# A delta-rule attention handed out in smaller pieces between the matmuls of a dense layer

## The chip, the cores and the metric

The kernel runs on one core of one Trainium2 chip. The metric is the device time of one execution in microseconds. Engines are named as in the profile: PE (TensorE matmuls), PEld (its weight loads), DVE (VectorE), ACT (ScalarE), POOL (GpSimd), SP (SyncE, which issues the DMAs).

## The reference

Three parts run one after the other on 4 x 768 tokens.

```
k_n = k / (norm(k) + 1e-6)                       # attention: B=4, H=8, S=768, D=48
for t in range(S):
    y[t] = q[t] @ state                          # per batch and head, state is D x D
    state += beta[t] * outer(k_n[t], v[t] - k_n[t] @ state)
x = y as (3072, 384)
x2 = leaky(x @ w_in, 0.01) @ w_out               # first dense layer, 384 -> 2048 -> 384
P = exp(x2 @ w_gate - max), 8 rounds of row and column normalising
out = sum_e P[:, e] * (relu(x2 @ w1[e]) @ w2[e]) # 8 experts, 384 -> 1024 -> 384
```

The arithmetic is that of 32-bit floats. Dense products are made of three products of a high and a low part each.

## The kernel before, in words

Time is cut into NT = 6 chunks of C = 128 tokens. For each chunk the recurrence becomes a triangular system per batch and head. `part1(t)` normalises k, makes its transpose (`kt_ps`), the products of k with itself (`g_ps`, two banks a batch) and their fp16 parts (`nh`, `nl`). `solve(t)` inverts the 32 x 32 (in chunks 0 and 1 the 16 x 16) diagonal blocks on DVE. `part2(t, b)` does one batch of one chunk: the masked products of k and q (`m_ps`, two halves), then the blocks `x` of the inverse, then levels that double the inverted blocks (s = 32 and 64; in chunks 0 and 1 also 16). A level is a first product (L284), ACT copies of it (L287), and the second products (L290, L294) with their copies. After the levels come a correction (`p_ps`, two pieces), `u_ps` (two pieces), the subtraction of the state's part from v (`ks_ps`), then w = u v (`w_ps`, 8 heads, L337), y (`y_ps`: the state's part L343 and the chunk's own part L346) and the state's update (`s_ps`, L354, with two DVE adds).

All three are Python generators. A `yield` marks the end of a piece, and a piece is what is handed out at once. `main_a(t)` runs the first dense layer on chunk t: 16 steps of 128 hidden columns over 512 tokens, each step three slots of three matmuls of `ph` (L503) and three slots of three matmuls of `po` (L555, for the step before). Chunk 0 has 20 steps, since its first LEAD = 4 hidden blocks go over two batches at a time. After each slot the loop gives credit: `ru` pieces from the queue of `part2` of chunk t + 1 (`bgq`, up to three generators in turn), `rs` from the queue of `part1(t + 2)` and `solve` (`bgs`), and in chunk 0 `rc` conversions. Shares are given by quarters (chunk 0: by sixths) of the step in `RATES` and `RATES0`. Before the next chunk's first step, `need_x1` hands out whatever is left of its `part2`, without slots between, and `make_x1` transposes y (L481). A batch b waits for batch b - 2, so two batches are open together, and both wait for `solve` of their chunk. `solve(t + 2)` waits for `part2` of chunk t + 1.

The weights of the first layer arrive as 64-bit floats. `convert()` turns 48 pieces of them into high and low parts on ACT, DVE and POOL (L431 to L460) and writes them to scratch in DRAM, from where `stage_a` reads them; where a step's weights are not converted yet, `stage_a` hands out the missing conversions itself. Both DMAs are issued by SP.

Ahead of the first step stands a start: `part1(0)`, `solve(0)`, and then a loop of 14 rounds (L619) that hands out one piece each of `part2(0, 0)`, `part2(0, 1)`, `part1(1)` and one conversion.

PSUM: `bank()` gives banks to the attention. In the start there are six, afterwards three (`bg`); two belong to `ph`, three to `po`. A bank comes free when its last reader is done.

The order in which a piece is handed out is a priority. A planner with its own costs puts the instructions of each engine into their order when the program is built; what it holds for not yet ready, it lets later ready work overtake. The experts run in an order that is written out by hand.

Of the kernel before, what the change touches and what calls it, by code (L numbers as in the profile page):

```python
# [8 lines left out]
F32 = mybir.dt.float32  # L9
# [4 lines left out]
ACTF = mybir.ActivationFunctionType  # L14
ALU = mybir.AluOpType
# [3 lines left out]
B, H, S, D = 4, 8, 768, 48  # L19
# [3 lines left out]
DM = H * D  # L23
# [18 lines left out]

STIR = (145, 20)

RATES0 = ((0.65, 0.3, 0.1), (0.7, 0.5, 0), (0.7, 0.45, 0), (1.05, 0.8, 0.4), (0.7, 0.35, 0), (1.05, 0, 0))
RATES = ((0.7, 0.5, 0), (0.7, 0.5, 0), (0.7, 0.5, 0), (0.7, 0.7, 0))


@with_exitstack
def delta_moe_kernel(ctx: ExitStack, tc: tile.TileContext, k_l, v_l, q_l, beta_l, wa_in, wg, wc, out):  # L50
# [3 lines left out]
    pe, act, dve, pool, sp = nc.tensor, nc.scalar, nc.vector, nc.gpsimd, nc.sync  # L54
# [21 lines left out]
    a1_p = attn_stack.enter_context(tc.tile_pool(name="a1", bufs=1, side="right"))  # L76
# [41 lines left out]
    def bank(name):  # L118
        if early is not None and early:
            early[0] += 1  # L120
            i = early[0] % 6
            if i >= 3:
                return po_p.tile([128, 512], F32, tag=f"po{i - 3}", name=name)
        return bg_p.tile([128, 512], F32, tag="bg", name=name)
# [3 lines left out]
    ybuf = {}  # L128
# [119 lines left out]
    def part2(t, b):  # L248
# [3 lines left out]
        mt = at_p.tile([128, H, C], F32, tag="mt", name="mt")  # L252
# [22 lines left out]
        for s in (16, 32, 64) if t in SMALL else (32, 64):  # L275
            pt = p1[b % 2]
            nb = C // (2 * s)

            def half(ap, odd):
                return ap.rearrange("p h (n two s) -> p h n two s", two=2, s=s)[:, :, :, odd, :]  # L280

            ps = bank("l_ps").rearrange("p (h n s) -> p h n s", h=H, n=nb)
            for h in range(H):
                marks.append(pe.matmul(out=ps[:, h], lhsT=nh[:, h, :], rhs=half(u, 1)[:, h], start=True, stop=True))  # L284
            for i in range(nb):
                o = 2 * s * i
                act.activation(out=pt[o:o + s, :, o + s:o + 2 * s], in_=ps[o:o + s, :, i, :], func=ACTF.Copy)  # L287
            ps = bank("l_ps").rearrange("p (h n s) -> p h n s", h=H, n=nb)
            for h in range(H):
                pe.matmul(out=ps[:, h], lhsT=x[:, h, :], rhs=half(pt, 1)[:, h], start=True, stop=True)  # L290
            if s > 16:
                ps2 = bank("l_ps").rearrange("p (h n s) -> p h n s", h=H, n=nb)
                for h in range(H):
                    pe.matmul(out=ps2[:, h], lhsT=pt[:, h, :], rhs=half(x, 0)[:, h], start=True, stop=True)  # L294
            for i in range(nb):
                o = 2 * s * i
                act.activation(out=u[o:o + s, :, o + s:o + 2 * s], in_=ps[o:o + s, :, i, :],  # L297
                               func=ACTF.Copy, scale=-1.0)
                if s > 16:
                    act.activation(out=x[o + s:o + 2 * s, :, o:o + s], in_=ps2[o + s:o + 2 * s, :, i, :],  # L300
                                   func=ACTF.Copy, scale=-1.0)
            if s == 16:
                dve.transpose(out=x.rearrange("p a b -> p (a b)"), in_=u.rearrange("p a b -> p (a b)"))
            yield
# [30 lines left out]
        ps = bank("w_ps")  # L335
        for h in range(H):
            pe.matmul(out=ps[:, h * D:(h + 1) * D], lhsT=uc[:, h, :], rhs=v[:, h, :], start=True, stop=True)  # L337
        act.activation(out=w, in_=ps[:, 0:DM].rearrange("p (h d) -> p h d", h=H), func=ACTF.Copy)
        yield
        ps = bank("y_ps")  # L340
        if t > 0:
            for p in range(NP):
                pe.matmul(out=ps[:, p * 2 * D:(p + 1) * 2 * D], lhsT=q[0:112, p, :],  # L343
                          rhs=st[0:112, b * NP + p, :], start=(p == 0), stop=False, skip_group_check=True)
        for h in range(H):
            pe.matmul(out=ps[:, h * D:(h + 1) * D], lhsT=mt[:, h, :], rhs=w[:, h, :],  # L346
                      start=(t == 0 and h == 0), stop=(h == H - 1), skip_group_check=True)
        y = a1_p.tile([128, DM], F32, tag=f"y{b}", name="y")
        act.activation(out=y, in_=ps[:, 0:DM], func=ACTF.Copy)
        ybuf[t, b] = y  # L350
        if t < NT - 1:
            ps = bank("s_ps").rearrange("p (n m) -> p n m", m=128)
            for p in range(NP):
                pe.matmul(out=ps[0:112, p, 0:2 * D],  # L354
                          lhsT=kn[:, 2 * p:2 * p + 2].rearrange("p a d -> p (a d)")[:, 0:112],
                          rhs=w[:, 2 * p:2 * p + 2].rearrange("p a d -> p (a d)"), start=True, stop=True)
            for o, c in ((0, 0), (64, D)):
                sv = st[o:o + D, b * NP:(b + 1) * NP, c:c + D]
                dve.tensor_tensor(out=sv, in0=sv, in1=ps[o:o + D, :, c:c + D], op=ALU.add)
        yield  # L360


# [213 lines left out]
    if True:  # L576
# [39 lines left out]
        run(s0)  # L616
        done.add(("s", 0))
        run(p1_1, 6)
        for _ in range(14):  # L619
            run(a0, 1)  # L620
            run(a1, 1)
            with tc.issue_after(solved[0].ins):
                run(p1_1, 1)
            run(cv_gen, 1)
# [459 lines left out]
```

## Time and profile before

| | us |
|---|---|
| median of three runs | 2488.13 |
| the runs | 2497.22, 2481.90, 2488.13 |
| profiled execution | 2491.82 |
| its span | 2489.8 |
| PE busy in the span | 2374.4 (95%) |
| DVE, ACT, POOL busy | 1263.4, 1162.8, 937.5 |

The stages, by the copies of the first layer's result (L560), are: the start to about 106 us, chunk 0 of the first layer to 320, chunks 1 to 4 to 847, chunk 5 with the first tiles of the experts to 940, and the experts to the end. In a row of the waits the left name is the instruction that waited and the right one what released it. Where these two share no operand, the wait is for a buffer. In a row of windows the clock is the share of TensorE's full clock that was granted; 0.50 is the lower of its two levels.

### The profile page before, as it was taken

The numbers are of one execution on the slowest core, as the hardware profiler recorded it, in microseconds if no ns is written. First come the engines' busy times: TensorE is split into PE (matmuls) and PEld (weight loads), VectorE is DVE, ScalarE is ACT, GpSimd is POOL, SyncE is SP. The second block draws the span as 40 slices with busy tenths as digits, with TensorE's granted clock in tenths as the row PEclk, the third lists the DMA queues.
The fourth block names the chain that finished last, engine by engine and source line by source line (L and its number), as shares of the span: only waits on it lengthen the run. The fifth ranks groups of instructions, "written<-read, shape, count | busy, mean of one in ns | idle before, by whom it ended". The sixth has DMA issues, their size and how long they took to land.

```text
span 2489.8 us, 35427 instructions
## 1 busy us (share of the span) xinstructions
PE 2374.4 (95%) x13836; PEld 2087.3 (84%) x13836; DVE 1263.4 (51%) x2320; ACT 1162.8 (47%) x2121; POOL 937.5 (38%) x966
## 2 busy tenths in 40 slices
PE   6788899999999999999999999999999999999999
PEld 5776677877877777899999999999999999999998
DVE  8567846446362357644444454444444544444444
ACT  6887666564654544433333344333333443333332
POOL 6435312132322213444434444444444443444441
PEclk7689999989899999999999999999999999999999
DMA  3355552424233552111111131111111311111111
GB/s 117 122 172 181 185 174 94 142 92 142 82 126 129 165 174 76 51 51 46 49 46 51 52 102 51 46 51 51 49 48 51 96 45 51 51 51 46 50 51 38
DMA packets 108695, 214.83 MB, mean 86 GB/s; under 512 B 11504, under 2 KB 79728, under 8 KB 108528
## 3 DMA queue, kind: packets, MB, share of 16 engines
q1 hardware_dynamic: 108528, 212.58, 27.5%
q8 instruction: 108, 1.77, 0.3%
q14 instruction: 59, 0.48, 0.1%
HBM read 190.43 MB, written 22.02 MB: 85 GB/s over the span
## 4 chain that ended last, share of the span: by engine, by line
PE 77%; ACT 10%; DVE 7%; issue 3%; DMA 2%; POOL 2%; SPq 0%; ACTq 0%; POOLq 0%; DVEq 0%
PE ye L964 32%; PE ph L880 13%; PE w L880 5%; PE y L880 5%; PE z L880 5%; PE ph L503 4%; PE po L555 4%; PE y_ps L346 2%; ACT x L271 2%; PE w_ps L337 2%; ACT a_d L205 1%; ACT p L287 1%; PE g_ps L189 1%; ACT u L297 1%; DVE tm L237 1%
## 5 line engine op out<-in xcount | busy, mean ns | idle before, releaser
L745 POOL TENSOR_TENSOR w2l<-stg,w2h 128x768 fp32r<-128x768 f32 x96 | 182.2, 1898 | 454.2 <-ACT w2h L744 454.2
L734 POOL TENSOR_TENSOR w1l<-stg,w1h 128x384 fp32r<-128x384 f32 x192 | 271.4, 1436 | 184.7 <-ACT w1h L733 167.2
L977 DVE SCALAR_TENSOR_TENSOR acc<-ye,pm,acc 128x384 f32<-128x384 f32 x168 | 103.5, 616 | 435.4 <-PE ye L964 435.4
L731 POOL TENSOR_TENSOR stg<-stg 128x128 f32<-128x128 f32 x384 | 209.0, 565 | 305.5 <-DMA stg<-wc 284.5
L890 ACT ACTIVATE xc<-ph 128x512 f32<-128x512 f32 x96 | 57.5, 599 | 448.5 <-PE ph L880 345.3
L555 PE MATMUL po<-gh,w 128*128 128x512 f32 (+1 forms) x600 | 217.3, 406 | 2.9 <-ACT gh L543 2.8
L880 PE MATMUL ph<-xoh,w1h 128*128 128x512 f32 x480 | 193.1, 402 | 4.7 <-DVE q L895 3.1
L503 PE MATMUL ph<-x1h,w 128*128 128x512 f32 (+1 forms) x600 | 186.7, 418 | 8.9 <-DVE leak L541 4.4
L895 DVE TENSOR_TENSOR q<-q,ph 128x512 f32<-128x512 f32 x192 | 132.2, 688 | 121.8 <-PE ph L880 121.8
L880 PE MATMUL ph<-xoh,w1l 128*128 128x512 f32 x480 | 188.1, 392 | 0.0
L880 PE MATMUL ph<-xol,w1h 128*128 128x512 f32 x480 | 187.7, 391 | 0.0
L733 ACT ACTIVATE w1h<-stg 128x384 fp32r<-128x384 f32 x192 | 121.1, 680 | 116.8 <-DMA stg<-wc 82.7
L541 DVE TENSOR_TENSOR leak<-leak,ph 128x512 f32<-128x512 f32 (+1 forms) x100 | 66.3, 663 | 165.7 <-ACT leak L540 165.5
L503 PEld LDWEIGHTS ph<-x1h,w 128*128 128x128 f32 x600 | 113.2, 202 | 32.5 <-DMA w<-wa_scratch 5.9
L555 PEld LDWEIGHTS po<-gh,w 128*128 128x128 f32 x600 | 115.4, 196 | 25.6 <-ACT gh L543 5.5
L545 POOL TENSOR_TENSOR gl<-leak,gh 128x512 fp32r<-128x512 f32 x48 | 62.1, 1294 | 192.4 <-ACT gh L543 174.7
L555 PE MATMUL po<-gl,w 128*128 128x512 f32 (+1 forms) x300 | 120.2, 401 | 3.8 <-POOL gl L545 2.3
L895 DVE TENSOR_TENSOR c<-xc,y 128x512 f32<-128x512 f32 x96 | 66.0, 688 | 106.2 <-PE y L880 83.1
L880 PEld LDWEIGHTS ph<-xoh,w1h 128*128 128x128 f32 x480 | 90.2, 188 | 34.4 <-DVE h31l L909 6.8
L880 PEld LDWEIGHTS ph<-xoh,w1l 128*128 128x128 f32 x480 | 90.2, 188 | 19.5
L540 ACT ACTIVATE leak<-ph 128x512 f32<-128x512 f32 (+1 forms) x100 | 57.8, 578 | 96.5 <-PE ph L503 93.8
L880 PEld LDWEIGHTS ph<-xol,w1h 128*128 128x128 f32 x480 | 90.3, 188 | 14.2
(316 smaller groups left out, 6683.7 us busy)
## 6 DMA issues: line engine op xcount, KB each, us to landing
w<-wa_scratch SPq DMA_DIRECT2D x100, 768.0 KB, 4.3
stg<-wc SPq DMA_DIRECT2D x192, 384.0 KB, 3.3
raw<-wa SPq DMA_DIRECT2D x48, 256.0 KB, 3.0
wa_scratch<-cvp SPq DMA_DIRECT2D x48, 256.0 KB, 2.5
stg<-x_scratch SPq DMA_DIRECT2D x10, 768.0 KB, 4.7
q<-q_l SPq DMA_DIRECT2D x24, 256.0 KB, 2.7
v<-v_l SPq DMA_DIRECT2D x24, 192.0 KB, 2.4
x_scratch<-x2o SPq DMA_DIRECT2D x18, 256.0 KB, 3.8
```

The source lines that it names most:

```text
L503: pe.matmul(out=ps, lhsT=wt[:, c * 128:(c + 1) * 128], rhs=xx[:, c], start=(n == 0), stop=(n == 3 * KD - 1))
L541: dve.tensor_tensor(out=g, in0=g, in1=ps, op=ALU.max)
L545: (dve if t in (0, 1, NT - 1) else pool).tensor_tensor(out=gl, in0=g, in1=fr(gh), op=ALU.subtract)
L555: pe.matmul(out=po[c][:, cols], lhsT=wt[:, DM + c * 128:DM + (c + 1) * 128], rhs=xx, start=(i == 1 and m == 0), stop=(i == n and m == 2), ...
L731: pool.tensor_tensor(out=s[:, o], in0=s[:, x], in1=s[:, y], op=op)
L733: ordered(act.activation(out=hi[:, j], in_=s[:, i], func=ACTF.Copy))
L734: pool.tensor_tensor(out=lo[:, j], in0=s[:, i], in1=fr(hi[:, j]), op=ALU.subtract)
L745: pool.tensor_tensor(out=lo, in0=s, in1=fr(hi), op=ALU.subtract)
L880: ordered(pe.matmul(out=ps, lhsT=w[:, a], rhs=x[:, b].rearrange("p s k -> p (s k)"), start=first, stop=i == 2 and (a, b) == terms[-1], ski ...
L895: ordered(dve.tensor_tensor(out=c, in0=x, in1=y, op=op))
L964: ordered(pe.matmul(out=ps[:, 0:DM], lhsT=xx[:, o:o + 128], rhs=wt, start=(f == 0 and i == 0), stop=(f == NF2 - 1 and i == 2), skip_group_ ...
L977: dve.scalar_tensor_tensor(out=a, in0=y, scalar=pm[:, t * B + b, e:e + 1], in1=a, op0=ALU.mult, op1=ALU.add)
```

## The change

A level's second products become a piece of their own. w is handed out as heads 0 to 2, 3 to 5, and 6 and 7 with the copy and the state's part of y; y's own part as heads 0 to 2, 3 to 5, and 6 and 7 with the copy. The state's update comes between the two parts of y, as its own piece, instead of behind y. With that `part2` has 19 pieces in chunks 2 to 4 instead of 12, 21 instead of 13 in chunks 0 and 1, and 18 instead of 12 in chunk 5. The first entries of the shares rise from 0.65, 0.7 and 1.05 to 0.95, 1.0 and 1.5. The start's loop has 22 rounds instead of 14, which also hand out 22 conversions instead of 14. No instruction is added or taken away.

```
--- before.py
+++ after.py
@@ -42,8 +42,8 @@
 
 STIR = (145, 20)
 
-RATES0 = ((0.65, 0.3, 0.1), (0.7, 0.5, 0), (0.7, 0.45, 0), (1.05, 0.8, 0.4), (0.7, 0.35, 0), (1.05, 0, 0))
-RATES = ((0.7, 0.5, 0), (0.7, 0.5, 0), (0.7, 0.5, 0), (0.7, 0.7, 0))
+RATES0 = ((0.95, 0.3, 0.1), (1.0, 0.5, 0), (1.0, 0.45, 0), (1.5, 0.8, 0.4), (1.0, 0.35, 0), (1.5, 0, 0))
+RATES = ((1.0, 0.5, 0), (1.0, 0.5, 0), (1.0, 0.5, 0), (1.0, 0.7, 0))
 
 
 @with_exitstack
@@ -285,6 +285,7 @@
             for i in range(nb):
                 o = 2 * s * i
                 act.activation(out=pt[o:o + s, :, o + s:o + 2 * s], in_=ps[o:o + s, :, i, :], func=ACTF.Copy)
+            yield
             ps = bank("l_ps").rearrange("p (h n s) -> p h n s", h=H, n=nb)
             for h in range(H):
                 pe.matmul(out=ps[:, h], lhsT=x[:, h, :], rhs=half(pt, 1)[:, h], start=True, stop=True)
@@ -335,28 +336,33 @@
         ps = bank("w_ps")
         for h in range(H):
             pe.matmul(out=ps[:, h * D:(h + 1) * D], lhsT=uc[:, h, :], rhs=v[:, h, :], start=True, stop=True)
+            if h % 3 == 2:
+                yield
         act.activation(out=w, in_=ps[:, 0:DM].rearrange("p (h d) -> p h d", h=H), func=ACTF.Copy)
-        yield
         ps = bank("y_ps")
         if t > 0:
             for p in range(NP):
                 pe.matmul(out=ps[:, p * 2 * D:(p + 1) * 2 * D], lhsT=q[0:112, p, :],
                           rhs=st[0:112, b * NP + p, :], start=(p == 0), stop=False, skip_group_check=True)
-        for h in range(H):
-            pe.matmul(out=ps[:, h * D:(h + 1) * D], lhsT=mt[:, h, :], rhs=w[:, h, :],
-                      start=(t == 0 and h == 0), stop=(h == H - 1), skip_group_check=True)
-        y = a1_p.tile([128, DM], F32, tag=f"y{b}", name="y")
-        act.activation(out=y, in_=ps[:, 0:DM], func=ACTF.Copy)
-        ybuf[t, b] = y
+        yield
         if t < NT - 1:
-            ps = bank("s_ps").rearrange("p (n m) -> p n m", m=128)
+            ss = bank("s_ps").rearrange("p (n m) -> p n m", m=128)
             for p in range(NP):
-                pe.matmul(out=ps[0:112, p, 0:2 * D],
+                pe.matmul(out=ss[0:112, p, 0:2 * D],
                           lhsT=kn[:, 2 * p:2 * p + 2].rearrange("p a d -> p (a d)")[:, 0:112],
                           rhs=w[:, 2 * p:2 * p + 2].rearrange("p a d -> p (a d)"), start=True, stop=True)
             for o, c in ((0, 0), (64, D)):
                 sv = st[o:o + D, b * NP:(b + 1) * NP, c:c + D]
-                dve.tensor_tensor(out=sv, in0=sv, in1=ps[o:o + D, :, c:c + D], op=ALU.add)
+                dve.tensor_tensor(out=sv, in0=sv, in1=ss[o:o + D, :, c:c + D], op=ALU.add)
+            yield
+        for h in range(H):
+            pe.matmul(out=ps[:, h * D:(h + 1) * D], lhsT=mt[:, h, :], rhs=w[:, h, :],
+                      start=(t == 0 and h == 0), stop=(h == H - 1), skip_group_check=True)
+            if h % 3 == 2:
+                yield
+        y = a1_p.tile([128, DM], F32, tag=f"y{b}", name="y")
+        act.activation(out=y, in_=ps[:, 0:DM], func=ACTF.Copy)
+        ybuf[t, b] = y
         yield
 
 
@@ -616,7 +622,7 @@
         run(s0)
         done.add(("s", 0))
         run(p1_1, 6)
-        for _ in range(14):
+        for _ in range(22):
             run(a0, 1)
             run(a1, 1)
             with tc.issue_after(solved[0].ins):
```

## Rows read from the trace of the kernel before

**Rows 1.** Windows: length; PE, PEld, DVE, ACT, POOL busy; clock, DMA, GB/s

```profile
0.00:106.00 106.00, 72.97 (x586) 62.70 (x587) 75.92 (x195) 75.33 (x155) 56.34 (x66) 0.70 0.37 117
106.00:320.00 214.00, 178.76 (x1432) 152.79 (x1433) 163.46 (x377) 158.03 (x371) 84.51 (x104) 0.86 0.57 182
320.00:940.00 620.00, 583.55 (x4066) 475.33 (x4065) 290.56 (x588) 339.09 (x607) 157.48 (x143) 0.95 0.39 130
940.00:2489.80 1549.80, 1539.14 (x7760) 1396.45 (x7758) 733.42 (x1161) 590.31 (x990) 639.15 (x653) 1.00 0.19 53
```

**Rows 2.** Waits of PE, 106 to 940: us in total, times, longest

```profile
PE l_ps L290 <- ACT p L287: 26.1, 33, 3.4
...
PE w_ps L337 <- ACT wv L338: 3.7, 3, 1.6
...
PE m_ps L256 <- ACT mt L260: 2.7, 3, 1.2
...
PE ks_ps L329 <- ACT uc L322: 2.2, 1, 2.2
...
PE g_ps L189 <- ACT mt L260: 2.2, 1, 2.2
```

**Rows 3.** Groups by line, 320 to 940: busy, mean ns, idle before, releaser

```profile
L290 PE MATMUL l_ps<-p,x 128*128 128x64 f16 x256 | 12.9, 194 | 12.9 <-ACT p L287 12.6
```

**Rows 4.** Windows, single stretches between 94 and 790

```profile
94.00:112.00 18.00, 17.21 (x83) 17.24 (x84) 5.95 (x18) 8.94 (x17) 6.05 (x6) 0.51 0.37 125
155.90:166.10 10.20, 10.15 (x49) 9.13 (x50) 4.33 (x10) 6.38 (x15) 2.19 (x4) 0.50 0.57 193
441.00:450.00 9.00, 9.00 (x80) 8.79 (x80) 5.15 (x14) 4.46 (x9) 0.00 (x0) 1.00 0.29 82
514.30:517.70 3.40, 1.82 (x14) 1.38 (x13) 2.05 (x5) 2.70 (x5) 0.55 (x1) 1.00 0.04 10
517.70:531.40 13.70, 13.70 (x59) 12.83 (x58) 2.85 (x10) 4.92 (x8) 3.94 (x3) 0.50 0.29 91
654.20:667.90 13.70, 13.70 (x58) 12.83 (x58) 2.63 (x10) 4.37 (x7) 4.29 (x3) 0.50 0.28 92
783.90:790.70 6.80, 6.80 (x27) 6.12 (x26) 0.00 (x0) 1.25 (x3) 1.27 (x1) 0.50 0.55 174
```

**Rows 5.** Timeline of PE, 509 to 534: start, us, what, idle before

```profile
516.47 2.55 PE L337 MATMUL w_ps<-v,uc 128*128 128x48 f32 x16 [1.58 <-ACT wv L338]
...
523.16 3.54 PE L346 MATMUL y_ps<-wv,mt 128*128 128x48 f32 x16
```

**Rows 6.** Timeline of all engines at the end of step 1

```profile
445.99 1.91 PE L346 MATMUL y_ps<-wv,mt 128*128 128x48 f32 x16
...
447.74 0.99 PE L354 MATMUL s_ps<-wv,kn 128*112 128x96 f32 x8
...
447.94 0.49 ACT L349 ACTIVATE y<-y_ps 128x384 f32<-128x384 f32 x1 [2.12 <-PE y_ps L346]
...
448.56 1.04 PE L481 MATMUL x_ps<-ident,y 128*128 128x128 f32 x8
...
449.36 0.48 PE L555 MATMUL po<-gh,w 128*128 128x512 f32 x1
```

**Rows 7.** Timeline of PE, 410 to 418: first and second product of a level

```profile
411.25 0.41 PE L284 MATMUL l_ps<-u,nh 128*128 128x64 f16 x8
411.49 0.48 PE L555 MATMUL po<-gh,w 128*128 128x512 f32 x1
...
412.27 0.62 PE L503 MATMUL ph<-x1h,w 128*128 128x512 f32 x2
414.38 0.39 PE L290 MATMUL l_ps<-p,x 128*128 128x64 f16 x8 [1.49 <-ACT p L287]
```

**Rows 8.** Groups by line, 106 to 320: a conversion's copy

```profile
L459 ACT ACTIVATE cvp<-cva 128x256 fp32r<-128x256 f32 x38 | 15.8, 414 | 10.7 <-POOL cva L447 10.2
```

## The prediction

> **What bounds the kernel now.** Read the stages first, PE's busy time and clock in each [rows 1]. From 940 us to the end the second mixture runs at full clock with PE busy 1539.1 of 1549.8 us, and no edited line runs there; I take it as fixed. All that can move lies before: PE idles 33.0 us ahead of 106, 35.2 us from 106 to 320, 36.5 us from 320 to 940, at mean granted clocks of 0.70, 0.86 and 0.95 [rows 1]. The list of PE's waits from 106 to 940 is headed by the second product of a level (L290) behind the ACT copy of the first: 26.1 us in 33 waits, 12.6 us of it after 320 [rows 2, 3]. Further down are waits of another sort: the releaser has nothing to do with the operands, it is the last reader of a PSUM bank. w behind an older w's copy, m_ps behind mt, ks_ps behind uc, g_ps behind mt: 3.7 + 2.7 + 2.2 + 2.2 = 10.8 us in 8 waits [rows 2]. Last, the clock. From 514.3 to 517.7 PE was busy 1.82 of 3.40 us, waiting for such a bank, and the next 13.7 us were granted 0.50, that is 1.2 instead of 2.4 GHz; 654 begins another such stretch [rows 4, 5]. At that clock the sixteen matmuls of y took 3.54 us, elsewhere 1.91 [rows 5, 6].
>
> **One thing about the order.** The program's order on PE is not the order of hand-out. Between the first and the second product of a level five dense matmuls (po, ph) have been put, though the old code has no hand-over there [rows 7]; and a po follows the eighth of twelve transposes of x, which are written in one go [rows 6]. So a planner already moves ready work into the places where it expects a wait. What is left of a wait is what it misjudged.
>
> **The terms**, against the profiled execution (2491.8 us; the median of the three runs, 2488.1, is 3.7 lower).
>
> 1. *Products apart.* What lies between the two products grows from the planner's choice to at least a slot of three dense matmuls (about 0.7 us by the spacing of those in [rows 7]), the other batch's eight small ones (0.24 us) and another slot. In the row shown 1.0 us lay between and 1.49 us of wait was left; some 1.6 us would leave about 0.9. The other waits are shorter, 26.1/33 = 0.8 us on average, so many go, but where ACT itself is behind (106 to 320: 158.0 of 214 us busy [rows 1]) more distance does not hurry it. Bounds: 0 and -26.1. I take half, **-13**.
>
> 2. *w and y in thirds.* Dense matmuls now stand inside the runs of 48-column matmuls. The low stretches in the middle of steps (517, 654, 784: 13.7 + 13.7 + 6.8 = 34.2 us, PE busy throughout [rows 4]) would at full clock be worth 17.1 us. The one at 517 began with PE idle behind a bank, which thirds do not cure; what they can do is end the low stretch sooner, since in it y and s ran with few dense matmuls between. Bounds 0 and -17.1; **-10**.
>
> 3. *Collections at a step's end.* This is the cost I see in the code. A batch of t>=2 was 12 pieces and an end, 13; now it is 19 and an end, 20 (the last chunk 19). Four batches: 52, then 80: times 1.54. The shares rise from 0.7 to 1.0: times 1.43. So it is not in proportion. Before x1 of the next chunk is wanted there are 90 slots. The solve's pieces open the batches at slot 25 (0.7 a slot in the last 6 slots of the step before, then 0.5). Of the pieces, 4 (the masks) are out by then. Old: 48/0.7 = 69 slots, to slot 94, so 2 or 3 pieces are collected in one go; new: 76, to slot 101, so 11. In step 1 the solve opens later still, at slot 33 instead of 27, since chunk 1's batches end at slot 98 of step 0 instead of 87: 19 pieces instead of 4. Steps 1 to 4: 4, 2, 2, 3 become 19, 11, 11, 8. Collected pieces have no slots between them. The 11 are s and y of two batches, which were collected before as well (441 to 450: PE busy 9.00 of 9.00 us, clock 1.00 [rows 4]): +1 us each for copies laid bare, +3. The 19 also hold ks, w and y·state, some 12 us of short matmuls in a row. Such a run ended the LEAD steps, and there 10.2 us of it had clock 0.50 [rows 4]: +5. In sum **+8**, bounds 0 and 4 x (1.6 + 5) = +26. The collection after the LEAD steps itself grows from 17 to 27 pieces, of 28 and 44: the same work, nothing.
>
> 4. *Banks held longer.* Three banks serve the background after the start. w's bank is now held over three pieces and y's over five, with the other batch's pieces and the slots between: during w and y a pair holds two of the three, and s_ps, kt_ps and the two g_ps of the next chunk share one. The nearest rows are the 8 bank waits, 1.35 us on average. Bounds: 0 (the planner fills in dense work) and rival 2's +38. I take three more such waits, **+4**, nearer the low end, since 8 in 834 us are few. The Trainium skill (TensorE: Matmul & The Clock Gate, "A second HAM failure mode: psum-queue depth-cycling") says that cycling PSUM banks makes PE idle briefly between groups and the clock swing between its two levels. The trace agrees at 514, where a bank wait of 1.58 us [rows 5] was followed by 13.7 us at 0.50; by that rule alone the term would be rival 2's.
>
> 5. *The state's update ahead of y.* s covered y's copy: its copy runs 447.94 to 448.43 under s, and the transposes start at 448.56 [rows 6]. With s first the copy lies bare, 0.5 to 0.8 us, at six ends, less what the planner fills in with the po of the step: **+2**, bounds 0 and +5. The earlier state gains nothing: no wait for the state's add stands in the list [rows 2]. Its add and ACT's copies are the same instructions as before.
>
> 6. *22 rounds instead of 14 in the start.* Eight conversions of weights (raw DMA, ACT, DVE, POOL, DMA out to scratch, all on SP's queue) move from the first 26 slots ahead of them. On ACT one costs up to four copies of 0.42 us (L431, L439, L446, L459) [rows 8], 8 x 1.6 = 13 us. The cover: in 94 to 112 w, y and s run at clock 0.51 and ACT is busy 8.9 of 18.0 us [rows 4]. Without the cover the start is up to 11 us longer, and LEAD's own waits for ACT are shorter by as much. **+1**, bounds -10 and +11. The chunk-1 pieces of the start stay in its first ten rounds.
>
> No instruction is added; hand-overs cost nothing on the chip. Sum: -13 - 10 + 8 + 4 + 2 + 1 = **-8**: 2484 for the profiled execution, **2480** as a median.
>
> **Rivals.**
> *1, all of it covered (0.22).* The waits of term 1 go and the middle low stretches too: -26 - 17 + 8 + 2 + 1 = -32, 2456. For it: in 320 to 940 those waits are shorter, 12.6 us in all, and little more distance would cover them. Against: ACT behind in the first step, and the falls began at waits that stay.
> *2, banks (0.18), slower.* With two of three banks held, g_ps, kt_ps and s_ps queue in PE's own order, and one wait is enough to halve the clock: 1.35 us and a low stretch of 6.8 us that costs 3.4, 4.75 together. Before the change 517 is such an event; two more in each of steps 1 to 4 are 8 x 4.75 = +38, with term 2 lost: -13 + 38 + 8 + 2 + 1 = +36, 2524. The gains of the rest are used up at the first of them; from the sixth on it is slower by over 1%. Against: before the change two g_ps already shared the banks with w, and it cost 3.7 us.
> *3, the planner makes the same of both (0.22).* Slots between products were there already [rows 7]; then only rounding is left, 2488.
>
> **The numbers.** The forecast has 0.38. About 1% (25 us) is what a measurement here can tell from no change; the three runs lie within 0.6%. Faster by over 1% is below 2463: rival 1 and little else, 0.24. Slower is above 2513: rival 2 and the upper bounds of terms 3 and 6, 0.17. Within: 0.59. The range reaches to both outer rivals, 2446 to 2525; the forecast's own is 2465 to 2498.
>
> **What would show it.** Term 1: L290's waits for ACT from 106 to 940 at 10 to 16 us. Term 2: low stretches in mid-step no longer than 7 us. Term 3: at the end of step 1 (about 450 us) a run of ks, w, s and y without ph between, with a fall of the clock. Term 4: bank waits of these four kinds 13 to 18 us. Term 5: x's transposes waiting for ACT's y. Wrong it is if the stage from 940 moves, if bank waits exceed 30 us, or if the start (to 106) shifts by over 10 us.

## The result and the profile after

The changed kernel takes **2502.14 us** in the median of seven runs (2493.45 to 2504.02), the one before 2483.20 in seven runs beside it (2475.14 to 2497.22). The ratio is **1.0064, 95% interval 1.0043 to 1.0085**: slower by some 16 us where 8 us less were forecast. The time lies inside the range; its sign does not agree.

The two profiled executions hide most of this. That of after took 2494.07 us and is the second fastest of its seven; that of before took 2491.82, which is above the median. They are 2 us apart. So the loss is read from all runs together. Each run has a span and a mean granted clock c of TensorE. In the tables **lost** is (1 - c) x span, what would come back if the whole span had full clock, and **rest** is the time without it. This is bookkeeping (a low clock while PE idles counts too), and c is given to 0.001, which is 2.5 us in a single run; the table has means. For before these are its 29 runs beside the first four experiments, since of the seven runs beside after only the times are on record.

| | runs | clock | lost | rest |
|---|---|---|---|---|
| before | 29 | 0.9651 | 86.7 | 2397.8 |
| after | 7 | 0.9589 | 102.8 | 2397.0 |

**The whole loss is clock**: +16.1 us lost, -0.8 us rest, in the means. The windows by stage of the kernel after, with the columns of [rows 1]:

```profile
0.00:106.00 106.00, 70.62 (x584) 61.47 (x585) 77.77 (x198) 77.04 (x157) 57.34 (x67) 0.71 0.36 115
106.00:320.00 214.00, 183.59 (x1408) 151.76 (x1408) 155.87 (x371) 152.97 (x365) 84.02 (x104) 0.83 0.54 176
320.00:940.00 620.00, 591.42 (x4081) 473.40 (x4081) 300.24 (x592) 337.07 (x611) 157.99 (x143) 0.95 0.39 131
940.00:2489.80 1549.80, 1541.19 (x7768) 1398.07 (x7766) 734.17 (x1161) 590.19 (x990) 638.41 (x653) 1.00 0.19 54
```

From 106 to 940 PE idles 30.4 + 28.6 = 59.0 us against 71.7 [rows 1]: 12.7 less. But from 106 to 320 the clock is 0.83 instead of 0.86, and PE is busy for 4.8 us longer there with fewer instructions (1408, not 1432): it is busy because it is slow. From 320 to 940 the clock is the same as before (0.95), so what these two traces show of the loss lies between 106 and 320. PE's busy time in the stage from 940 agrees with before to 2 us. Behind these windows stand the waits of PE from 106 to 940, as in [rows 2]:

```profile
PE m_ps L256 <- ACT mt L260: 8.7, 5, 3.3
PE l_ps L284 <- ACT u L298: 7.5, 10, 2.1
PE w_ps L338 <- DVE v L334: 6.6, 7, 2.0
PE l_ps L295 <- ACT u L298: 5.8, 9, 2.2
PE l_ps L291 <- ACT p L287: 5.1, 7, 1.4
PE ks_ps L330 <- ACT uc L323: 4.8, 1, 4.8
...
PE x_ps L487 <- ACT y L364: 0.5, 1, 0.5
```

The head of the old list is gone: the second product of a level (L291 now) waits 5.1 us, not 26.1. New in the list is w (L338) behind v, which DVE makes: 6.6 us in 7 waits, all from 300 on; before, from 300 to 940, it was 1.8 us in 4. What such a wait does is seen in PE's timeline after (start, us, what, idle before), to be held against [rows 5]:

```profile
567.53 1.03 PE L330 MATMUL ks_ps<-state,kT 112*128 112x96 f32 x8
...
569.11 1.03 PE L330 MATMUL ks_ps<-state,kT 112*128 112x96 f32 x8
...
572.83 0.84 PE L338 MATMUL w_ps<-v,uc 128*128 128x48 f32 x6 [1.97 <-DVE v L334]
...
575.00 1.49 PE L338 MATMUL w_ps<-v,uc 128*128 128x48 f32 x6
576.27 1.20 PE L509 MATMUL ph<-x1h,w 128*128 128x512 f32 x2
577.27 1.35 PE L338 MATMUL w_ps<-v,uc 128*128 128x48 f32 x6
578.41 1.63 PE L509 MATMUL ph<-x1l,w 128*128 128x512 f32 x3
579.83 1.35 PE L338 MATMUL w_ps<-v,uc 128*128 128x48 f32 x6
580.97 1.63 PE L509 MATMUL ph<-x1h,w 128*128 128x512 f32 x3
...
587.45 1.70 PE L351 MATMUL s_ps<-wv,kn 128*112 128x96 f32 x8
588.95 4.39 PE L359 MATMUL y_ps<-wv,mt 128*128 128x48 f32 x20
```

w waits 1.97 us and runs in thirds with two or three dense matmuls between each until 583. From 583.1 to 597.2 what is left of w, y and s runs with no dense matmul between: it is the collection at the end of step 2 (step t is the first layer on chunk t). The windows of the whole stretch, of this collection and of the one of step 3, which has as many matmuls (71 in the trace) at full clock:

```profile
573.90:601.20 27.30, 27.30 (x118) 25.51 (x117) 10.05 (x22) 10.18 (x18) 2.73 (x4) 0.50 0.21 63
583.10:597.20 14.10, 14.10 (x71) 14.10 (x70) 4.83 (x8) 7.67 (x14) 1.26 (x1) 0.50 0.23 66
727.80:735.20 7.40, 7.40 (x71) 7.40 (x70) 3.48 (x7) 7.06 (x13) 1.27 (x1) 1.00 0.43 124
```

PE is busy for all of 27.3 us at a clock of 0.50, and half of that is the collection. The stretches at 517 and 654 before were 13.7 us each [rows 4]. The length of such a stretch does not follow from the wait: w waits 1.95 us for v at 718 too, and there 6.8 us of low clock follow (from 720.7, behind another 0.34); the other four waits of w for v, of up to 0.87 us, are followed by none. Why v is late is on DVE's timeline of after (same columns):

```profile
565.86 1.38 DVE L239 TENSOR_TENSOR xs<-xs,tm 128x231 f32<-128x231 f32 x1
567.27 0.39 DVE L237 TENSOR_TENSOR tm<-ld,xs 128x220 f32<-128x220 f16 x1
...
570.83 0.32 DVE L239 TENSOR_TENSOR xs<-xs,tm 128x156 f32<-128x156 f32 x1
571.07 0.55 DVE L332 TENSOR_TENSOR v<-v,ks_ps 128x384 f32<-128x384 f32 x1
571.53 0.68 DVE L547 TENSOR_TENSOR leak<-leak,ph 128x512 f32<-128x512 f32 x1
572.13 0.55 DVE L334 TENSOR_TENSOR v<-v,beta 128x384 f32<-128x384 f32 x1
573.06 1.32 DVE L237 TENSOR_TENSOR tm<-ld,xs 128x135 f32<-128x135 f16 x1
```

ks_ps of the two open batches ends at 568.56 and 570.14. Instructions of the next chunk's solve (tm and xs) go first until 571.15, and a leak of the dense layer stands between the two instructions that make the first v; it is there at 572.68, and w starts 0.15 us later.

### The profile page after: what moved, and what is told of

Same layout as the page of the kernel before. It is cut to its first block, busy times and chain, and to the rows that moved or that the text cites. A ratio compares the mean times of both kernels' runs of the same rounds, so it can differ in the third digit from the quotient of the medians.

```text
span 2492.3 us, 35437 instructions
## 1 busy us (share of the span) xinstructions
PE 2386.8 (96%) x13836; PEld 2084.7 (84%) x13836; DVE 1268.0 (51%) x2320; ACT 1157.3 (46%) x2121; POOL 937.8 (38%) x966
## 3 DMA queue, kind: packets, MB, share of 16 engines
q1 hardware_dynamic: 108528, 212.58, 27.3%
## 4 chain that ended last, share of the span: by engine, by line
PE 66%; DVE 2%; DMA 1%; ACT 1%; issue 0%; POOL 0%; SPq 0%; ACTq 0%; POOLq 0%; DVEq 0%
PE ye L970 32%; PE ph L886 13%; PE y L886 5%; PE w L886 5%; PE z L886 5%; PE po L561 2%; PE ph L509 2%; DMA stg<-wc 0%; PE y_ps L359 0%; PE w_ps L338 0%; DMA w<-wa_scratch 0%; DVE pm L869 0%; POOL w1l L740 0%; DMA stg<-x_scratch 0%; POOL stg L737 0%
## 5 line engine op out<-in xcount | busy, mean ns | idle before, releaser
L561 PE MATMUL po<-gh,w 128*128 128x512 f32 (+1 forms) x600 | 227.3, 412 | 4.5 <-ACT gh L549 4.4
L509 PEld LDWEIGHTS ph<-x1h,w 128*128 128x128 f32 x600 | 112.0, 205 | 26.3 <-DVE leak L547 5.0
L546 ACT ACTIVATE leak<-ph 128x512 f32<-128x512 f32 (+1 forms) x100 | 57.9, 579 | 122.4 <-PE ph L509 118.2
L886 PEld LDWEIGHTS ph<-xol,w1h 128*128 128x128 f32 x480 | 90.5, 188 | 14.1
```

Of the source, the lines that this page charges most:

```text
L509: pe.matmul(out=ps, lhsT=wt[:, c * 128:(c + 1) * 128], rhs=xx[:, c], start=(n == 0), stop=(n == 3 * KD - 1))
L561: pe.matmul(out=po[c][:, cols], lhsT=wt[:, DM + c * 128:DM + (c + 1) * 128], rhs=xx, start=(i == 1 and m == 0), stop=(i == n and m == 2), ...
L886: ordered(pe.matmul(out=ps, lhsT=w[:, a], rhs=x[:, b].rearrange("p s k -> p (s k)"), start=first, stop=i == 2 and (a, b) == terms[-1], ski ...
```

## The experiments

Fifteen kernels, in four groups that shared their runs of the kernel before. Each table row gives the ratio to before with its interval, the number of runs, and lost and rest as above. The medians and the lost time of before were 2487.29 and 86.7 us (first group), 2486.20 and 86.5, 2477.67 and 82.8, 2483.12 and 83.6.

### Which part loses the clock

Four kernels, each the changed one with one part altered. **e1_shares** raises the first shares to 1.65 (chunk 0) and 1.58 times (later) those of before, as the pieces grew, so that little is left to collect; **e2_whole** hands out w and y whole, with shares and rounds to suit (18 rounds, so 18 conversions); **e3_levels_whole** keeps a level's products together (19 rounds and conversions); **e4_start** hands out only 14 conversions in the 22 rounds.

```
e1: RATES0 firsts 1.073, 1.155, 1.155, 1.732, 1.155, 1.732; RATES firsts 1.106
e2: -            if h % 3 == 2:      (in w and in y)
    -                yield
    -        for _ in range(22):
    +        for _ in range(18):     RATES0 firsts x 0.91 (the first of them 0.89), RATES firsts x 0.875
e3: -            yield               (behind the copies of L287)
    +        for _ in range(19):     RATES0 firsts x 0.994 (the first of them 0.97), RATES firsts x 1.001
e4: +            if i < 14:
    +                run(cv_gen, 1)
```

> The changed kernel with shares raised a little more (times 1.65 in chunk 0 and 1.58 after it over the kernel before, instead of 1.43 to 1.46), so that 4, 4, 4 and 1 pieces are left to be collected at the ends of steps 1 to 4 instead of 19, 11, 11 and 8. Theory C (the loss is the collections, where short matmuls run in a row): the 27 us at the lower clock that begin at 574 go, and the time falls to the kernel before or under it, ratio 0.995 to 1.000. Theory T (thirds of w and y keep the clock low, whoever stands between): ratio stays at 1.004 to 1.009 and low stretches of over 13 us are still there. Theory S (the fuller start): stays at 1.004 to 1.009, with chunk 0 as in the changed kernel.

> The changed kernel with w and y whole again (levels still apart, the state's update still ahead of y; 18 rounds in the start, shares times 1.3 and 1.25, so that 5, 3, 3 and 0 pieces are collected). Theory T: without thirds the low stretches in mid-step fall back to the before's or shorter while the waits saved at the levels stay, ratio 0.993 to 1.000. Theory C: the same as the run with more shares, 0.995 to 1.000, so that the two runs do not differ by over 0.2%. Theory S: ratio about 1.003, half of the start's extra conversions being gone.

> The changed kernel with a level's products in one piece again (w and y in thirds, the state's update ahead; 19 rounds, shares times 1.42 and 1.43; 5, 3, 3 and 0 pieces collected). The waits of the second product for its first's copy come back, some 20 us from 106 to 940, and the new ones of the next level's first product for u's copy (7.5 us) and of the third (5.8 us) go. Theory T: slowest of the four, ratio 1.005 to 1.012, since it keeps the thirds and loses the gain. Theory C: 1.000 to 1.005. Theory that the levels apart are the loss: 0.995 to 1.000.

> The changed kernel with 14 conversions in the start's 22 rounds instead of 22. Theory S: the part to the end of chunk 0's first layer is 5 to 10 us shorter than in the changed kernel (328), and the ratio falls to 1.001 to 1.004. Theories C and T: nothing, 1.004 to 1.009; the start and the first steps trade the eight conversions evenly.

| | ratio [95%] | runs | lost | rest |
|---|---|---|---|---|
| e1_shares | 1.0084 [1.0060, 1.0109] | 6 | 107.8 | 2400.2 |
| e2_whole | 0.9979 [0.9961, 0.9996] | 12 | 89.3 | 2392.2 |
| e3_levels_whole | 1.0006 [0.9990, 1.0021] | 12 | 85.3 | 2401.7 |
| e4_start | 1.0022 [0.9999, 1.0045] | 12 | 82.5 | 2405.8 |

**The collections are not the cause**: with 4, 4, 4 and 1 pieces left to collect, where after has 19, 11, 11 and 8, e1 is no faster, and its lost time is the highest of all (though higher shares change more than the collections). In the kernel after, the collection of 19 that was feared runs at full clock:

```profile
441.00:452.00 11.00, 11.00 (x100) 10.89 (x99) 6.96 (x21) 2.52 (x6) 0.00 (x0) 1.00 0.51 156
```

At step 2 a collection stood in the low clock (583.1 to 597.2 above, 14.1 us instead of 7.4), but the fall came ahead of it.

The three others each bring most of the clock back, though each undoes another part. So the parts do not add up. One thing the three have in common: with 18, 19 and 14 conversions they all take back some of the eight that after hands out early. What e4 undoes is seen in the windows from 112 to 180, the first LEAD steps, one fence each for before, after and e4:

```profile
112.00:180.00 68.00, 56.83 (x459) 49.87 (x458) 49.79 (x121) 55.71 (x141) 27.91 (x40) 0.75 0.57 180
```

```profile
112.00:180.00 68.00, 56.90 (x423) 48.38 (x423) 46.03 (x117) 49.36 (x126) 27.35 (x38) 0.70 0.49 157
```

```profile
112.00:180.00 68.00, 54.86 (x453) 46.77 (x452) 51.28 (x125) 52.92 (x136) 27.68 (x39) 0.80 0.50 159
```

PE is as busy after as before, with 36 instructions fewer and the clock at 0.70; with 14 conversions it is 0.80 and nearly the old count. (The profiled execution of e4 is the fastest of its twelve, 2473.23 us where their median is 2488.27.) But e4's rest is 9 us higher, so its time is only 0.4% below that of after.

### Pieces in pairs; levels alone; the state's update

If a piece after every slot is what loses the clock (theory P), handing out twice the share after every second slot (**e5_pairs**, on after) brings it back. If the levels are enough, **e6_levels_alone** shows it: the kernel before with nothing but the new hand-over, 17 rounds, the old 14 conversions and shares of about 0.83. **e7_whole_start** is e2 with 14 conversions. **e8_state_behind** is after with the state's update put back behind y.

```
e5: -                bgq.spend(ru, 3)
    +                bgq.spend(2 * ru * (n % 2), 3)
e6: +            yield               (before, behind the copies of L287)
    +        for i in range(17):     RATES0 firsts x 1.25, RATES firsts x 1.18
    +            if i < 14:
    +                run(cv_gen, 1)
e7: +            if i < 14:          (on e2)
    +                run(cv_gen, 1)
e8: s_ps, its products and adds      (moved behind ybuf[t, b] = y and a yield)
```

> The changed kernel with attention handed out after every second slot, two slots' shares at once. All pieces, thirds and the sum of the shares stay; only the six dense matmuls of two slots now stand together. So far the mean granted clocks of all runs put the changed kernel's loss in the clock: 0.9589 against 0.9651, 16 us of lost time, and the rest equal (2397.0 and 2397.8 us). Theory P (a short piece after every slot is the pattern in which the clock does not recover): clock back to 0.963 to 0.968, ratio 0.997 to 1.002. Rival B (w's and y's banks held over many pieces make the idle in which the clock falls): clock stays at 0.957 to 0.961, ratio 1.004 to 1.009.

> The kernel before with a level's products apart and nothing else (17 rounds in the start with the old 14 conversions, shares times 1.25 and 1.18; 4, 2, 3 and 3 pieces collected). Theory P: the shares stay well under one piece a slot, so the clock stays at 0.964 to 0.967, and the waits of the second product shrink by some 15 us and come back in part at the next level: ratio 0.994 to 0.999. Rival (splitting the levels is itself a cause of the low clock): clock under 0.962, ratio 1.002 to 1.006.

> The run with w and y whole (ratio 0.998, clock 0.964, rest 2392 us) with 14 conversions instead of 18 in the start. If the extra conversions cost clock in the start and the first steps as they seemed to (0.9668 against 0.9589 with 14 instead of 22, but 9 us more in the rest), the ratio is 0.994 to 0.997; if they only move work, it stays at 0.997 to 0.999.

> The changed kernel with the state's update behind y again, still a piece of its own. If the update ahead of y lays y's copy bare and holds y's bank longer, the ratio falls from 1.006 to 1.002 to 1.004, by less idle and fewer falls at the steps' ends; if the order of the two has no part in it, it stays at 1.004 to 1.009 with a clock of 0.957 to 0.961.

| | ratio [95%] | runs | lost | rest |
|---|---|---|---|---|
| e5_pairs | 1.0070 [1.0043, 1.0097] | 7 | 100.0 | 2401.3 |
| e6_levels_alone | 1.0085 [1.0056, 1.0113] | 6 | 102.6 | 2401.9 |
| e7_whole_start | 1.0018 [0.9998, 1.0038] | 12 | 95.4 | 2393.7 |
| e8_state_behind | 1.0046 [1.0023, 1.0068] | 12 | 99.3 | 2395.9 |

P falls: pairs recover nothing. **Levels alone cost as much as the whole change** (e6), with the old conversions and whole w and y. e7 is 0.4% above e2, the intervals just apart: with w and y whole, four conversions fewer gain nothing, so what e4 gave back belongs to a kernel with thirds and 22 rounds and is no price of a conversion as such. e8's interval overlaps that of after, so what the place of the state's update is worth stays open; it is small. The trace of e6 has the same event as after: the wait, the run of w behind it, and the windows that follow.

```profile
PE w_ps L338 <- DVE v L334: 5.3, 3, 2.2
```

```profile
574.93 3.62 PE L338 MATMUL w_ps<-v,uc 128*128 128x48 f32 x16 [2.06 <-DVE v L334]
```

```profile
320.00:940.00 620.00, 588.61 (x4090) 474.67 (x4089) 297.37 (x614) 337.08 (x609) 156.82 (x143) 0.94 0.39 133
574.90:595.40 20.50, 20.47 (x85) 19.34 (x86) 9.54 (x25) 2.67 (x6) 1.51 (x2) 0.50 0.22 70
721.70:731.90 10.20, 10.20 (x44) 9.62 (x43) 4.39 (x14) 0.98 (x2) 0.00 (x0) 0.50 0.23 70
800.20:817.30 17.10, 17.10 (x67) 15.19 (x66) 0.00 (x0) 2.10 (x4) 1.27 (x1) 0.50 0.24 72
```

From 300 to 940 the low clock that begins at a wait of w is 58.0 us in e6 (10.2 of it behind a bank) and 64.9 in e1. In after it is 34.1, all behind v; in before it is also 34.1, 27.3 behind a bank (at 517 and 654) and 6.8 behind v (at 784); in e2 20.5, in e4 6.8, in e3 none. These are single executions, that of e1 the slowest of its six.

### v ahead of u

Theory V: w's wait for a late v starts the low stretches of steps 1 to 4. Its test takes the wait away without touching any other edit: the pieces of ks and v are handed out ahead of those of u, so v is ready two pieces sooner. Nothing is left out. **e9_v_early** does it on after, **e10_levels_v_early** on e6, **e12_whole_v_early** on e2, and **e11_before_v_early**, as a control, on before.

```
+        w = at_p.tile(...)          # and ks_ps, v - ks, v * beta, yield
+        ...
         uc = at_p.tile(...)         # u_ps, two pieces
         ...
-        w = at_p.tile(...)          # and ks_ps, v - ks, v * beta, yield
-        ...
         ps = bank("w_ps")
```

> The changed kernel with the subtraction and scaling of v (ks_ps and its two DVE operations) handed out ahead of the two u pieces, so two pieces earlier. Theory V: in the changed kernel w waits for v, because v stands in DVE's queue behind the solve of the next chunk (6.6 us in 7 waits from 300 to 940, 1.8 in 4 before), and a wait at that place is the dear one: only short matmuls follow it, and the low clock lasts 10 to 27 us. With v early these waits fall under 2 us, the low stretches behind a wait of w under 10 us (34 now), clock 0.962 to 0.966, ratio 0.999 to 1.003. Rival (the place does not matter, the number of waits does; w then waits for uc instead): clock 0.957 to 0.961, ratio 1.004 to 1.009.

> The kernel before with the levels apart alone (ratio 1.0085, clock 0.9590, 58 us of low clock behind waits of w), and v handed out two pieces earlier. Theory V: w's waits for v (5.3 us in 3) and the low stretches behind them go, clock 0.964 to 0.967, ratio 0.997 to 1.002. Rival: stays at 1.006 to 1.011.

> The control: the kernel before with v handed out two pieces earlier. There w waits for v 1.8 us in all, and its two long low stretches stand behind waits for a bank (w behind the older w's copy), which this does not touch. Theory V: ratio 0.997 to 1.002, clock 0.963 to 0.967. Rival (v early is a gain or a loss by itself): outside of that.

> The run with w and y whole (ratio 0.998, clock 0.9640, rest 2392 us, 4.5 us of waits of w for v, 20 us of low clock behind waits of w), and v handed out two pieces earlier. Theory V: some 5 to 10 us of clock come back, ratio 0.993 to 0.997. Rival: unchanged, 0.997 to 1.000.

| | ratio [95%] | without it | runs | lost | rest |
|---|---|---|---|---|---|
| e9_v_early | 1.0064 [1.0039, 1.0090] | after 1.0064 | 6 | 98.4 | 2395.4 |
| e10_levels_v_early | 0.9981 [0.9959, 1.0004] | e6 1.0085 | 12 | 81.3 | 2395.1 |
| e11_before_v_early | 0.9926 [0.9903, 0.9948] | before 1 | 6 | 75.4 | 2384.1 |
| e12_whole_v_early | 0.9928 [0.9906, 0.9950] | e2 0.9979 | 12 | 70.9 | 2390.6 |

For the levels V came out as forecast: 1.0085 becomes 0.9981, lost 102.6 becomes 81.3. But the move gains on before too (e11), and with v early on both sides the levels still cost 0.55% (0.9981 against 0.9926, intervals apart): 5.9 us of clock, where without it they cost 16.1, and 11.0 of rest. So V is shown for some 10 us of the levels' clock, and not for all that they cost. The window of e10 beside that of e6 above (0.94):

```profile
320.00:940.00 620.00, 590.73 (x4205) 473.65 (x4204) 314.20 (x638) 353.13 (x641) 167.07 (x151) 0.98 0.42 139
```

The control missed. Before had little wait for v, and yet the move gains 0.7% there; the waits of w for a bank (3.7 us, [rows 2]) are gone from its list as well, low clock behind a wait of w falls from 34.1 to 3.4 us, and 14 us of rest go too. They are idle time of PE: from 106 us to the end of the first layer PE idles 57.1 us in e11 (busy 731.46 of 788.60) and 71.4 in before (busy 747.97 of 819.40). Both **e11 and e12 beat both kernels**, and they are alike: what e12 keeps of the change (products apart, the state ahead of y, 18 rounds) gives and costs nothing in sum once v is early. That e10, with the products apart alone, stands 0.5% above both is not explained. In e12 the low clock behind waits of w is still 17.1 us (behind uc and a bank) where e2 has 20.5, so its gain is not shown to be V's.

On the whole change the move gains nothing (e9), and that V did not expect. In the profiled run the low clock of steps 1 to 4 fell from 57.9 to 27.0 us, but step 0 grew from 216.2 to 226.6 us, with 86.7 us of low clock instead of 66.0. PE's timeline of e9, and two of its windows:

```profile
223.00 0.58 PE L333 MATMUL u_ps<-u,x 128*128 128x128 f16 x4 [3.33 <-ACT uc L334]
```

```profile
205.00:250.00 45.00, 40.10 (x227) 34.11 (x227) 25.75 (x62) 29.54 (x61) 20.83 (x24) 0.70 0.47 151
222.20:246.10 23.90, 21.76 (x94) 19.48 (x94) 9.99 (x23) 15.93 (x34) 11.52 (x14) 0.50 0.42 132
```

The second half of u waits 3.33 us for the copy of an earlier half (a bank), and 23.9 us of low clock follow. In e9 ACT's conversions and parts of chunk 2 stand ahead of that copy.

### The first steps or the later thirds

What is left of the loss in e9 against e12 is the thirds, and the start that comes with them. Theory F puts it in the start and the first step, theory G in the thirds of the later steps. All have v early, levels apart and the state ahead. **e13_thirds_late** has thirds from chunk 2 on alone, with e12's 18 rounds and first shares. **e14_thirds_first** has them in chunks 0 and 1 alone, with 22 rounds and e12's later shares. **e15_start_14** is e9 with 14 conversions in the 22 rounds.

```
e13: +            if h % 3 == 2 and t > 1:     (w and y; 18 rounds)
e14: +            if h % 3 == 2 and t < 2:     (w and y; RATES firsts 0.875)
e15: +            if i < 14:
     +                run(cv_gen, 1)
```

> The changed kernel with v early, and w and y in thirds only from chunk 2 on, with 18 rounds and chunk 0's shares as in the runs with w and y whole. With v early the changed kernel keeps its ratio (1.0064) although steps 1 to 4 have lost their long low stretches (27 us of low clock, 58 before); in its profile the start and the first step stand at 338.6 us against 321.2 with w and y whole and v early (0.9928). Theory F (the rest of the loss is the start and the first step with thirds and 22 rounds): ratio 0.993 to 0.999, clock 0.966 to 0.970. Rival G (it is the thirds and the 19, 11, 11, 8 collected pieces of steps 1 to 4): stays at 1.003 to 1.008.

> The complement: v early, thirds only in chunks 0 and 1 with the changed kernel's 22 rounds and first shares, and w and y whole from chunk 2 on with shares times 1.25. Theory F: ratio 1.002 to 1.007, clock 0.959 to 0.964. Rival G: 0.993 to 0.998.

> The changed kernel with v early and 14 conversions in its 22 rounds. If within the start and the first step it is the conversions that cost (their ACT and DVE work ahead of the first steps), the ratio falls to 0.996 to 1.001; if it is the thirds there, it stays at 1.003 to 1.008.

| v early, and | later steps whole | later steps in thirds |
|---|---|---|
| first steps whole, 18 rounds | e12 0.9928 [0.9906, 0.9950] | e13 0.9967 [0.9945, 0.9989] |
| first steps in thirds, 22 rounds | e14 1.0003 [0.9983, 1.0023] | e9 1.0064 [1.0039, 1.0090] |

e15 is 1.0003 [0.9983, 1.0024]. Lost and rest: e13 76.0 and 2398.3, e14 97.2 and 2385.7, e15 79.0 and 2404.1; twelve runs each.

The first steps' edit costs 0.75 to 0.97% (down the columns), the later thirds 0.39 to 0.61% (along the rows; for the smaller the two intervals just overlap). F carries more, G is not nothing, and e14 lies between what the two had forecast. The two costs are of different kinds: the first steps' edit is all clock (lost +26.3 and +22.4 us, rest -4.9 and -2.9), the later thirds are mostly rest (+7.7 and +9.7, lost +5.1 and +1.2). Of F, the eight conversions alone are 0.61% (e9 against e15): 19.4 us of clock, with 8.7 us of rest gained. The event at 222 of e9 comes again in e14, with the same edit of the first steps, in PE's timeline and a window:

```profile
223.55 0.59 PE L333 MATMUL u_ps<-u,x 128*128 128x128 f16 x4 [2.99 <-ACT uc L334]
```

```profile
223.10:247.00 23.90, 22.11 (x95) 19.73 (x95) 10.36 (x24) 15.81 (x33) 11.16 (x13) 0.50 0.43 138
```

It is missing from e13 and e15; the same 45 us as in e9, at 0.98 and 0.99 instead of 0.70:

```profile
205.00:250.00 45.00, 39.90 (x301) 33.50 (x302) 35.28 (x79) 38.34 (x78) 25.12 (x28) 0.98 0.59 192
```

```profile
205.00:250.00 45.00, 39.33 (x290) 32.36 (x289) 36.84 (x83) 35.81 (x75) 23.74 (x26) 0.99 0.59 194
```

## Why the prediction was wrong

**What failed first is term 6**, eight more conversions in the start at +1 us, covered by an idle ACT in 94 to 112. The cover was there and was not used: in before and in after ACT had ended eleven conversions by 112 (their last copy is L459 before, L465 after), and the start before the first step is 112.1 us against 111.5. The eight do not run earlier afterwards either (24 ended by 180 in after and in e4, 25 in before). They only stand ahead of the LEAD steps' attention in the order, and from there on the price falls: by 180 fewer PE instructions and a lower clock, and with v early the wait of 3.33 us at 222. They cost 0.4% in after (1.0064 against e4's 1.0022, whose intervals just touch) and 0.6% with v early (e9 against e15, apart). That is 10 to 15 us, at the bound of +11 and past it. Both pairs split alike: 20.3 and 19.4 us of clock lost, 8.8 and 8.7 us of rest gained. That is more clock than the whole change loses (16.1). All six kernels with 22 conversions lose 97 to 108 us of clock; the eleven with 14 to 19 lose 71 to 95, except e6 (102.6). That the place of the eight in the order lowers the clock is shown for kernels with thirds and 22 rounds; by which waits is seen in single traces only.

**Term 2 failed too**, w and y in thirds at -10 us. The prediction said of the dense matmuls between the thirds that "what they can do is end the low stretch sooner". By themselves they did not. In e1, which has the thirds and only one piece left to collect at the end of that step, a low stretch runs on for 20.5 us through thirds and dense matmuls by turns, with PE busy throughout (a piece of the timeline, then the window):

```profile
817.30 1.35 PE L359 MATMUL y_ps<-wv,mt 128*128 128x48 f32 x6
818.44 1.63 PE L509 MATMUL ph<-x1h,w 128*128 128x512 f32 x3
819.87 0.92 PE L359 MATMUL y_ps<-wv,mt 128*128 128x48 f32 x4
```

```profile
803.90:824.40 20.50, 20.50 (x73) 18.18 (x73) 0.69 (x1) 3.25 (x7) 1.63 (x2) 0.50 0.26 84
```

The bounds of the term went from 0 to -17.1, with none on the side of a loss. With v early the later thirds cost 0.39 to 0.61%, 10 to 15 us, so the term was wrong in sign there. In after itself, undoing all thirds gives 0.85% back (e2), but e2 takes back four of the eight conversions with them, and so the two are not separated.

**Term 1 came out right in the sum, in part by luck.** PE's idle time fell by 12.7 us, and 13 were forecast for this term alone. But the waits of the levels' products fell by 8.0 us only (L284 and L290 before, 26.4; L284, L291 and L295 behind p and u after, 18.4). The rest of the 12.7 left other waits, such as ph's for a DMA (4.4 to 0.6) and g_ps's for kT (5.3 to 1.1), while m_ps's for mt grew. The line that answers to [rows 3]:

```profile
L291 PE MATMUL l_ps<-p,x 128*128 128x64 f16 x256 | 13.0, 194 | 0.2 <-ACT p L287 0.2
```

The wait at L291 went further than thought (26.1 to 5.1, with 10 to 16 forecast), and others came in its place: L284 and L295 behind u, m_ps behind mt. What the term left out is the clock: the levels alone are +0.85% (e6), 16.1 us of it clock, and some 10 us of that clock goes with w's wait for v (e10 and e11). A sum of idle time saw the 26 us at L290, and not that the two longest low stretches of before began elsewhere.

**Term 3 had a price of the right size in the wrong place.** At the end of step 1, where a fall was forecast, the collection ran at full clock (441 to 452). At the end of step 2 one ran in the low clock, 14.1 us where step 3 took 7.4: 6.7 us, where +5 were put on step 1. But the fall came from the wait ahead of it, and a kernel with few pieces left to collect is no faster (e1).

**Term 4 was right in its sum.** The four kinds of bank waits are m_ps 8.7 + ks_ps 4.8 + w_ps 0 + g_ps 0 = 13.5 us (13 to 18 forecast). They are 6 waits instead of 8, though, where three more were forecast, and none is for a bank that w or y held, so the sum is partly luck. The Trainium skill (TensorE: Matmul & The Clock Gate, "A second HAM failure mode: psum-queue depth-cycling") was set beside this term for the swings of the clock. The traces agree in part: the falls at 517 and 654 of before and at 222 of e9 stand behind bank waits, those at w in after behind an operand, v, that is late.

**Term 5** was too small to matter: one wait of x's transposes for y, 0.5 us.

**Rival 2** had the sign, and neither the size (+36, where it is some +16) nor the place. It put falls of the clock behind bank waits in steps 1 to 4. In after 17.1 us of low clock there stand behind bank waits (of m_ps, at 328, 543 and 687) and 34.1 behind w's waits for v, and from 320 to 940 the clock is no lower than before (0.95). The stretch at 573.9 is worth 27.3 / 2 = 14 us, where the rival took 3.4 for each. Rival 1 is excluded by the sign, rival 3 by the interval.

What stays open: whether undoing levels (e3) or thirds (e2) mends the changed kernel by itself, or by the three and four conversions that go back with it, and why e7, with four conversions fewer than e2, is slower. Each edit moves the places where PE meets a late ACT or DVE. That taking such a wait away brings clock back was tested for w at v alone (e10); for u at 222 the wait and the low clock come and go together (in e9 and e14, not in e13 and e15).

## What to carry to other kernels

When a background stream is handed out between dense matmuls, do not judge a hand-out by the sum of idle time: look at which wait stands ahead of a run of short matmuls, and whether the low clock behind it is longer than the wait. Split the time of many runs into clock and rest first; single profiled executions can hide or make a difference of this size. Have the operands of such a run ready some pieces before it (here v ahead of u, worth 0.5 to 1% in three of four kernels). Work that is handed out earlier "into a gap" goes ahead in the queue whether or not the gap takes it, so ask whom it stands in front of (here 10 to 15 us, where +1 was forecast).

## What the runs showed of the hardware

**More of the spread is in the granted clock than in the rest.** Between kernels rest moves by 22 us in all and lost by 37. Over the runs of before rest has a standard deviation of 3 to 4 us and lost of 8 to 10; in the other kernels it is 2.0 to 4.6 and 3.4 to 9.7.

**Dense matmuls between short ones did not by themselves bring the clock back**: 20.5 us at 0.50 with PE busy 20.50 us, dense and short matmuls by turns (e1, 803.9 to 824.4).

**DVE stands still beside POOL.** In the DVE rows above, xs (231 columns) took 1.38 us and tm (135 columns) 1.32, where tm of 220 columns took 0.39. POOL's timeline of the same stretch:

```profile
565.66 1.32 POOL L551 TENSOR_TENSOR gl<-leak,gh 128x512 fp32r<-128x512 f32 x1 [7.23 <-ACT gh L549]
572.96 1.28 POOL L551 TENSOR_TENSOR gl<-leak,gh 128x512 fp32r<-128x512 f32 x1 [4.20 <-ACT gh L549]
```

Both long ones began within 0.2 us behind a gl and ended 0.1 to 0.3 us after it. The Trainium skill (SBUF — State Buffer, "SBUF: two separate sides") says that a DVE instruction with two SBUF inputs and a GpSimd instruction that reads SBUF hold a shared pair of ports by turns, each for a whole instruction. The trace agrees: about 1 us is added to each. The second gl did not touch the first v, which was done before it began. The first gl may have: DVE has no gap of over 0.04 us from the long xs to v, so up to 1 us of v's lateness can come from it; no run separates that.
